# Opening of an attention and feed-forward kernel: products that alternate between heads, a second transposed buffer, another order of loads

## The chip, the cores and the metric

The kernel runs on one core of a Trainium2 chip. Its time is device microseconds of one execution. Three executions of the kernel before took 940.44, 939.76 and 935.5 us (median 939.76). The profile is of one more execution.

A core has five engines with queues of their own: PE (matrix products; its weight loads are listed as PEld), DVE (vector), ACT (scalar), POOL (GpSimd) and SP, which here only issues DMAs. PE writes to PSUM, which has banks of 512 columns of 4 bytes; DVE and ACT read PSUM and SBUF, POOL works in SBUF.

## The reference

Masked attention for 8 batches and 8 heads (576 positions, 64 columns each), then a feed-forward layer with a gate over all 4608 positions:

```python
scores = scale * np.matmul(q, k.transpose(0, 1, 3, 2))
mask_local = (rel >= 0) & (rel < stride)
mask_strided = (rel >= 0) & (pos[None, :] % stride == pos[:, None] % stride)
...
scores = scores - np.max(scores, axis=-1, keepdims=True)
attn = np.exp(scores)
attn = attn / (np.sum(attn, axis=-1, keepdims=True) + 1e-09)
...
h = x @ w_in
relu6 = np.clip(h + 3.0, 0.0, 6.0)
g = h * relu6 / 6.0
return (g @ w_out).astype(np.float32)
```

The stride is 32. Heads 0 to 3 use the local mask, heads 4 to 7 the strided one. The feed-forward layer goes from 512 columns to 2048 and back.

## The kernel before

**Pairs and chunks.** Heads are worked two at a time. A pair g is batch b and chunk c (0 to 3, two heads each); chunks 0 and 1 are local, 2 and 3 strided. In batch 0 the order of the chunks is 0, 2, 1, 3. The text calls them pair 0, pair 2, pair 1 and pair 3, by their chunk; names of tiles carry batch and chunk: `ps_00` is a score bank of batch 0, chunk 0.

**A pair.** Queries and keys are loaded, transposed, and multiplied to scores in two PSUM banks, one per head. A masking product with the identity lies below them. Then come the maximum of each row, its subtraction, the exponential, the sum, its inverse, and the normalising product. The probabilities are transposed and multiplied with the values (`pv`), and `keep_x` (L401) splits the result into a high and a low part, `x`, for the feed-forward products; ACT casts the high part, DVE subtracts to get the low one. The last 64 positions of each batch go to tiles `left`.

The code of `kept_pair` (L427) serves the pairs of batches 0 and 1; later pairs have `pair` (L774). Within `kept_pair`, the pairs of batch 0 are `early`: they load and transpose queries and keys on PE (L475, L482), have more PSUM banks to choose from, and take the maximum straight from PSUM, negated (`most_of`, L619). PE then adds that to the scores in the bank (`less_of`, L622), and ACT reads the bank for the exponential (`exp_of`, L626). Local pairs of batch 0 are also `shifted`: their probabilities are transposed on PE (`turned`, L705), and copied back (L710, L712) to a tile `at`. Their products with the values (`both`, L714) run over one head, 18 blocks of 32 positions, then over the other. Strided pairs transpose their probabilities on DVE (L693), each head into the same zeroed tile `atkept`: the second head's transposes follow the first head's products (`mm`, L743).

**Feed-forward.** For each batch's 512 main positions, and for the left ones, 16 hidden chunks: `ph` gets four groups of three products (high and low parts of x and w_in, L1033 to L1035; one group for each chunk c of x), ACT and DVE apply the gate, ACT and POOL split it (`gh`, L1057, and `gl`, L1062), and three products per output bank go into `acc` (L991 to L993). For batch 0, the first four hidden chunks are begun together.

**Weights.** `weight_part` (L293) loads each 128x512 piece (L306) and splits it: two ACT passes (L314, L318), a DVE join (L322), a cast on ACT or POOL (L328, L330), a subtraction on POOL (L334).

**Order.** `Plan` (L54) collects all operations with their costs and due times, and `emit` (L84) writes them out in the order in which a list schedule with these costs would start them. So costs and due times decide what stands where on each engine's queue, and any change of them can move rows anywhere behind it. Engines work their queues in order. The calls that the change touches give due times to loads (`op("SP", ...)`, L336, L497, L542). Where the plan sees PE idle early, it puts in idle products (`idle`, L1134).

Of the kernel before, what the change touches and what calls it, by code (L numbers as in the profile page):

```python
# [33 lines left out]
TURNS = ((0, 2, 1, 3), (2, 3, 0, 1)) + ((0, 2, 1, 3),) * 6  # L34
AHEAD = 27.0
# [139 lines left out]
def attention_ffn(ctx: ExitStack, tc, q, k, v, w_in, w_out, out):  # L175
# [117 lines left out]
    def weight_part(k, w, g, i):  # L293
# [42 lines left out]
        op("SP", 0.53, load, writes=[key], due=-49 + 0.01 * k if k < 6 else -2 + 0.1 * k if k < 16 else due - 20.0, early=7.0 if k < 16 else due - 30.0, after=1.6 if k < 16 else 1.25)  # L336
# [90 lines left out]
    def kept_pair(g):  # L427
# [7 lines left out]
        slow = 1.7 if g == 0 else 1.1 if early else 1.0  # L435
# [26 lines left out]
        for x in "qk":  # L462
# [6 lines left out]
            if early:  # L469

                def load(x=x, nkey=nkey):
                    t = new(wp, nkey, [P, RUN, 2, D], F32, f"{x}n{nm}")
                    rows = {"q": q, "k": k}[x][b, h0:h0 + 2].rearrange("j (p i) d -> p i j d", i=RUN)
                    for part in (slice(0, D), slice(D, S // RUN)):
                        (nc.scalar if g == 1 else nc.sync).dma_start(t[part], rows[part])  # L475
# [21 lines left out]
                op("ACT" if g == 1 else "SP", 0.9, load, writes=[nkey], due=-60 + 2 * g + (x == "k") - 900 * (g == 1), after=1.15)  # L497
                op("PE", 0.126 * RUN * (1.1 if g else 1.6), tr, words=4 * RUN, reads=[("ident",), nkey, "plain", tkey[x]], writes=tb, take=tb, due=due - 1020, mode="s")
# [43 lines left out]
        op("SP", 1.8 if loc else 2.0, load_v, writes=[vkey, skey] if shifted else [vkey], due=-48.8 if g == 1 else -54.5 + 2 * g if early else due - 30, early=0 if early else due - 35, after=3.0 if shifted else 2.0)  # L542
# [3 lines left out]
        akeys = [("atl", j) for j in range(2)] if loc else [wkey("o", NQ - 1, 0)] * 2  # L546
# [50 lines left out]
        def keep(e, j):  # L597
# [3 lines left out]
            if e == "ACT":  # L601
                nc.scalar.copy(e_both()[:, j], ps)
            else:
                nc.vector.tensor_copy(e_both()[:, j], ps)
        both_halves = [x + (1,) if isinstance(x, tuple) else x + "1" for x in (qkey, kkey)]
        sd = due - 12
        op("PE", (2.0 if loc else 1.75) * slow, scores, reads=["const", qkey, kkey, *both_halves], writes=[*sb, stkey] if early else [*sb, ekey, ekey + "1", stkey],
           take=sb, due=sd - 1000, room=0.0 if early else ROOM, mode="s", words=4 * 2 * (18 if loc else 32) + 6)
        for j in range(0 if early else 2):
# [6 lines left out]
        def most_of(j):  # L616
            if j == 0:
                new(ap, stkey, [P, 2, 2, 8], F32, f"st{nm}")
            nc.vector.tensor_reduce(out=st_of(0)[:, j], in_=ps_of(j), axis=AX.X, op=ALU.max, negate=True)  # L619

        def less_of(j):
            nc.tensor.matmul(ps_of(j), tiles["ident",][:n, :n], st_of(0)[:, j].unsqueeze(2).to_broadcast([n, nblk, w]),  # L622
                             start=False, stop=True, skip_group_check=True)

        def exp_of(j):
            nc.scalar.activation(e_own(j), in_halves(ps_of(j)), AF.Exp, scale=SCALE)  # L626
# [29 lines left out]
        if early:  # L656
            for j in range(2):
                op("DVE", 0.18 + 0.00105 * cols, partial(most_of, j), reads=[sb[j]], writes=[stkey] if j == 0 else [stkey + (1,)], due=sd + 0.7)
            for j in range(2):
                op("PE", 0.0018 * cols * slow, partial(less_of, j), reads=[stkey if j == 0 else stkey + (1,), ("ident",)], writes=[sb[j]], due=sd - 999, mode="l", words=4)  # L660
            for j in range(2):
                op("ACT", 0.2 + 0.00085 * cols, partial(exp_of, j), reads=[sb[j]], writes=[ekey] if j == 0 else [ekey + "1"], give=sb[j], due=sd + 1.5)
# [19 lines left out]
        def transposes(j):  # L682
            def tr():
                at, e = tiles[akeys[j]], e_whole(j)
# [10 lines left out]
            op("DVE", 6 * 0.37 if loc else 4 * 0.435, tr, reads=[ekey, ekey + "1"], writes=[akeys[j]], due=due - 2 + j)  # L695
# [478 lines left out]
```

## Time and profile before

| | |
|---|---|
| median of 3 runs | 939.76 us |
| the profiled execution's own time | 940.2 us |
| its span, first to last instruction | 938.4 us |
| mean granted PE clock | 0.993 |
| POOL, share of the span | 44% |
| DVE, share of the span | 63% |
| moved by DMA | 57.60 MB, 61 GB/s over the span |

In the tables by stage and in the timelines, times are us from the span's start. A timeline row has the start, the length, the engine, the line, the operation, what is written and read with its size, the count of merged instructions, and in brackets the idle time before and what ended it. A busy PE may be running products that take longer than their work needs, so its 98% is no measure of what could be saved.

### The profile page before, as it was taken

Reading aid. Unit: us, or ns where it says so; the run is one execution under the profiler, and the core shown is the slowest. Engines: PE = TensorE matmul, PEld = TensorE weight load, DVE = VectorE, ACT = ScalarE, POOL = GpSimd, SP = SyncE. Lnnn points to the kernel's source line nnn. Section 1 sums busy time; section 2 is a strip of 40 time slices with the busy share of each in tenths; the row PEclk is TensorE's granted clock in tenths of the full one; section 3 lists DMA queues with packets and bytes.
Section 4 is the critical chain, followed back from the end, with each engine's and each line's share of the span. In section 5 each row is a group of like instructions: output and inputs, shape, how many; then the busy total and the mean of one; then the engine's idle time right before and its main releaser. Section 6 shows DMA issues by size and latency. Waiting matters only on the chain.

```text
span 938.4 us, 16352 instructions
## 1 busy us (share of the span) xinstructions
PE 922.1 (98%) x5741; PEld 762.4 (81%) x5741; DVE 590.3 (63%) x1604; ACT 491.0 (52%) x1214; POOL 417.0 (44%) x398
## 2 busy tenths in 40 slices
PE   7989999999999999999999999999999999999997
PEld 5778788888888888988888888888888888888896
DVE  4677968677877765556476778777887675111111
ACT  1657657655565546456356555655556563322332
POOL 3468675544444434433354444454454452222221
PEclk9979999999999999999999999999999999999999
DMA  9978522321222022023013222322223200100100
GB/s 147 329 164 240 144 58 43 77 49 29 53 71 42 15 56 71 1 49 55 14 29 84 40 42 40 83 44 42 40 42 78 49 1 14 45 1 1 39 8 23
DMA packets 194394, 57.60 MB, mean 61 GB/s; under 512 B 185032, under 2 KB 185032, under 8 KB 194312
## 3 DMA queue, kind: packets, MB, share of 16 engines
q1 hardware_dynamic: 191960, 55.97, 26.3%
q10 hardware_dynamic: 2352, 0.59, 0.4%
q8 instruction: 45, 0.74, 0.3%
q14 instruction: 37, 0.30, 0.1%
HBM read 47.09 MB, written 9.44 MB: 60 GB/s over the span
## 4 chain that ended last, share of the span: by engine, by line
PE 93%; DMA 2%; SPq 2%; DVE 1%; issue 1%; POOL 1%; ACT 0%; POOLq 0%
PE acc L991 13%; PE ph L1033 13%; PE acc L993 12%; PE acc L992 12%; PE ph L1034 12%; PE ph L1035 12%; PE ps L868 3%; PE pv L398 2%; PE phl L1033 2%; PE phl L1035 2%; PE phl L1034 2%; PE accl L993 2%; PE accl L991 2%; PE accl L992 2%; PE pv L943 1%
## 5 line engine op out<-in xcount | busy, mean ns | idle before, releaser
L1062 POOL TENSOR_TENSOR gl<-u,gh 128x512 fp32r<-128x512 f32 x128 | 169.8, 1327 | 267.1 <-ACT gh L1057 242.8
L1033 PE MATMUL ph<-x,wi 128*128 128x512 f32 x512 | 202.2, 395 | 0.0
L991 PE MATMUL acc<-wo,gh 128*128 128x512 f32 x512 | 202.1, 395 | 0.0
L993 PE MATMUL acc<-wo,gl 128*128 128x512 f32 x512 | 200.2, 391 | 0.3 <-POOL gl L1062 0.3
L1034 PE MATMUL ph<-x,wi 128*128 128x512 f32 x512 | 200.2, 391 | 0.0
L1035 PE MATMUL ph<-x,wi 128*128 128x512 f32 x512 | 200.0, 391 | 0.0
L992 PE MATMUL acc<-wo,gh 128*128 128x512 f32 x512 | 199.8, 390 | 0.0
L1045 ACT ACTIVATE u<-ph,three 128x512 f32<-128x512 f32 x128 | 88.2, 689 | 190.9 <-PE ph L1035 190.0
L1049 DVE SCALAR_TENSOR_TENSOR u<-u,ph 128x512 f32<-128x512 f32 x128 | 87.6, 685 | 126.5 <-ACT u L1045 124.9
L892 ACT ACTIVATE e<-e,st 96x128 f32<-96x128 f32 (+2 forms) x264 | 102.7, 391 | 43.9 <-DVE st L886 43.3
L993 PEld LDWEIGHTS acc<-wo,gl 128*128 128x128 f32 x512 | 96.1, 188 | 22.0 <-POOL gl L1062 1.3
L1035 PEld LDWEIGHTS ph<-x,wi 128*128 128x128 f32 x512 | 96.4, 188 | 20.7
L991 PEld LDWEIGHTS acc<-wo,gh 128*128 128x128 f32 x512 | 96.1, 188 | 19.6
L1033 PEld LDWEIGHTS ph<-x,wi 128*128 128x128 f32 x512 | 96.4, 188 | 18.9 <-DVE u L1049 0.5
L992 PEld LDWEIGHTS acc<-wo,gh 128*128 128x128 f32 x512 | 96.2, 188 | 17.8
L1034 PEld LDWEIGHTS ph<-x,wi 128*128 128x128 f32 x512 | 96.5, 188 | 16.7
L1057 ACT CAST gh<-u 128x512 fp32r<-128x512 f32 x128 | 79.3, 621 | 57.3 <-DVE u L1049 52.0
L908 POOL TENSOR_TENSOR e<-e,st 96x96 f32<-96x96 f32 (+1 forms) x72 | 68.4, 963 | 81.1 <-DVE st L903 74.9
L886 DVE CUSTOM_DVE_ANT_0 e<-ps,e 96x128 f32<-96x128 f32 (+2 forms) x264 | 63.4, 279 | 2.2
L925 DVE STREAM_TRANSPOSE atstr<-e 32x160 f32<-32x160 f32 x168 | 56.3, 335 | 7.2 <-POOL e L908 4.5
L925 DVE STREAM_TRANSPOSE atloc<-e 32x192 f32<-32x192 f32 (+1 forms) x144 | 52.1, 362 | 9.4 <-POOL e L908 7.1
L418 DVE TENSOR_TENSOR x<-pv,x 128x512 fp32r<-128x512 f32 (+3 forms) x48 | 31.7, 660 | 36.6 <-ACT x L415 24.2
(154 smaller groups left out, 1378.6 us busy)
## 6 DMA issues: line engine op xcount, KB each, us to landing
rawi<-in_moe_w_in_dram SPq DMA_DIRECT2D x16, 512.0 KB
rawo<-in_moe_w_out_dram SPq DMA_DIRECT2D x16, 512.0 KB
out_dram<-ob SPq DMA_DIRECT2D x32, 256.0 KB
qn<-in_q_dram SPq DMA_DIRECT2D x112, 72.0 KB
kn<-in_k_dram SPq DMA_DIRECT2D x112, 72.0 KB
vt<-in_v_dram SPq DMA_DIRECT2D x24, 160.0 KB
vt<-in_v_dram SPq DMA_DIRECT2D x120, 31.5 KB
v<-in_v_dram SPq DMA_DIRECT2D x16, 72.0 KB
```

Source lines behind the costliest of these rows:

```text
L892: nc.scalar.activation(e, e, AF.Exp, bias=st_of(j, 0)[:, i:i + 1], scale=-1.0, accum_out=st_of(j, 1)[:, i:i + 1])
L925: nc.vector.transpose(at[ks, i0:, qs], e[qs, i0:, ks])
L991: nc.tensor.matmul(acc, gh, woh, start=fc == 0, stop=False)
L992: nc.tensor.matmul(acc, gh, wol, start=False, stop=False)
L993: nc.tensor.matmul(acc, gl, woh, start=False, stop=end)
L1033: nc.tensor.matmul(ph, wih, xh, start=n_ == 0, stop=False)
L1034: nc.tensor.matmul(ph, wih, xl, start=False, stop=False)
L1035: nc.tensor.matmul(ph, wil, xh, start=False, stop=n_ == NCC - 1)
L1045: nc.scalar.activation(u, tiles[pk][:, :n], AF.Relu, bias=three)
L1049: nc.vector.scalar_tensor_tensor(out=u, in0=u, scalar=6.0, in1=tiles[pk][:, :n], op0=ALU.min, op1=ALU.mult)
L1057: nc.scalar.copy(g, tiles[uk][:, :n])
L1062: eng.tensor_tensor(out=g, in0=tiles[uk][:, :n], in1=tiles[gk[0]][:, :n].bitcast(F32), op=ALU.subtract)
```

## The change

Five things change, all for the pairs of batch 0.

- **Products with the values.** In local pairs, `both` now takes blocks of the two heads in turn. Each bank gets 9 blocks of either head (288 positions) in place of 16 and 2. `keep_x` reads the banks in three pieces.
- **A second buffer for strided pairs.** The second head's probabilities go to two tiles of their own (`at1`), zeroed once on DVE, so both heads' transposes may precede all products, which `both_mm` issues in turn by head. Eight transposes of 128 columns are issued for the second head in place of four of 256.
- **Maximum and subtraction.** Scores are copied from PSUM to SBUF (`keep`, as in later pairs). The maximum is taken there, POOL subtracts it, and the exponential works in place. PE's L622 products are gone. Local pairs do this by head, strided pairs for both heads at once.
- **Loads.** Due times of loads come from lists. SP's queue now has the queries of pairs 0 and 2, the values of pair 0, two pieces of w_in, queries and keys of pair 1, two more of w_in, the values of pair 2, queries and keys of pair 3, the values of pair 1. ACT issues the keys of pairs 0 and 2, where it issued queries and keys of pair 2. Before, the queries and keys of all four pairs and the values of pairs 0 and 1 stood ahead of the first weight.
- **Costs** in the plan of early pairs and loads.

The diff, cut to its core:

```diff
+FIRST = (-57.0, -53.9, -56.5, -53.8)
+QK = (-60.0, -59.0, -55.0, -52.0)
+VAL = (-56.0, -53.0, -51.0, -49.0)
...
-        slow = 1.7 if g == 0 else 1.1 if early else 1.0
+        slow = (1.75, 1.75, 1.6, 1.3)[g] if b == 0 else 1.0
...
-                        (nc.scalar if g == 1 else nc.sync).dma_start(t[part], rows[part])
+                        (nc.scalar if g < 2 and x == "k" else nc.sync).dma_start(t[part], rows[part])
...
         def most_of(j):
-            if j == 0:
-                new(ap, stkey, [P, 2, 2, 8], F32, f"st{nm}")
-            nc.vector.tensor_reduce(out=st_of(0)[:, j], in_=ps_of(j), axis=AX.X, op=ALU.max, negate=True)
+            nc.vector.tensor_reduce(out=st_of(0)[:, j].rearrange("p (h u) -> p h u", h=2), in_=e_own(j), axis=AX.X, op=ALU.max)
 
         def less_of(j):
-            nc.tensor.matmul(ps_of(j), tiles["ident",][:n, :n], st_of(0)[:, j].unsqueeze(2).to_broadcast([n, nblk, w]),
-                             start=False, stop=True, skip_group_check=True)
+            x = e_own(j)
+            nc.gpsimd.tensor_tensor(out=x, in0=x, in1=in_halves(st_of(0)[:, j].unsqueeze(2).to_broadcast([n, nblk, w])), op=ALU.subtract)
...
-        if early:
+        if shifted:
             for j in range(2):
...
+                if akeys[j] == "at1":
+                    for a in range(4):
+                        rows = slice(PAD * a, PAD * a + PAD)
+                        for h in range(2):
+                            nc.vector.transpose(tiles["at1", h][rows, :, rows], e[rows, 4 * h:4 * h + 4])
+                    return
...
-                for j in range(2):
-                    own = slice(D * j, D * j + D)
-                    for u in range(3 * NQB):
-                        n0 = PAD * u
...
+                half = 3 * NQB // 2
+                for h in range(2):
+                    for x in range(half):
+                        for j in (h, 1 - h):
+                            own = slice(D * j, D * j + D)
+                            bank = (h + j) % 2
+                            u = x + half * bank
+                            n0 = PAD * u
...
+            def both_mm():
+                ps, vt = [psum(vb[h], f"pv{nm}{h}") for h in range(2)], tiles[vkey]
+                for i in range(8):
+                    for j in range(2):
+                        at = tiles["at1", i // 4][:, i % 4] if j else tiles[akeys[0]][:, i]
+                        nc.tensor.matmul(ps[i // 4][D * j:D * j + D, i % 4 * P:i % 4 * P + 4 * NPOS], vt[:, j, i],
+                                         at.rearrange("p (a m) -> p a m", a=4)[:, :, :NPOS], start=True, stop=True)
...
+    def at1(e):
+        for h in range(2):
+            t = tiles["at1", h] = new(xp, ("x", 1, 2, h), [P, 4, P], F32, f"at1{h}")
+            on(e).memset(t, 0.0)
+    op(either(1.1), 0, at1, writes=["at1", ("x", 1, 2, 0), ("x", 1, 2, 1)], due=9)
```

How rows move, at three places. The numbers of lines are each kernel's own. PE at pair 0's products with the values, before (`pv_00` and `pv_01` are the two banks):

```order
L722 MATMUL pv_00_510<-at_0_466,v_0_179 64x32 x16
L722 MATMUL pv_01_511<-at_0_466,v_0_179 64x32
L722 MATMUL pv_01_511<-at_0_466,vlast 64x32
L722 MATMUL pv_00_510<-at_0_466,v_0_179 64x32 x16
L722 MATMUL pv_01_511<-at_0_466,v_0_179 64x32
```

and now, where pair 1's scores already stand ahead of them:

```order
L486 MATMUL qp_30_543<-ident,qn_3_315 128x72 x4
L486 MATMUL qp_31_544<-ident,qn_3_315 128x72 x4
L734 MATMUL pv_00_568<-at_0_458,v_0_172 64x32
L734 MATMUL pv_01_569<-at_0_458,v_0_172 64x32
L734 MATMUL pv_00_568<-at_0_458,v_0_172 64x32
L734 MATMUL pv_01_569<-at_0_458,v_0_172 64x32
```

One head's 18 blocks in a row have become blocks of two heads in two banks by turns.

POOL from the normalising of pair 0's probabilities on (`e`; `st_2` are the row values of pair 2, `st_1` those of pair 1; `wi` and `fi` are pieces of w_in), before:

```order
L634 TENSOR_TENSOR e<-e,st_0_328 96x2x3x64 x2
L458 MEMSET qt_2_456 128x32x14
L653 TENSOR_TENSOR e<-e,st_2_451 128x2x8x18
L330 CAST wi_555<-fi_483 128x512
L522 MEMSET v_2_605 128x1024
L334 TENSOR_TENSOR wi_555<-fi_483,wi_555 128x512
```

and now:

```order
L636 TENSOR_TENSOR e<-e,st_0_307 96x2x3x64 x2
L462 MEMSET qt_2_423 128x32x14
L640 TENSOR_TENSOR e<-e,st_2_417 128x2x8x18
L333 CAST wi_430<-fi_405 128x512
L337 TENSOR_TENSOR wi_430<-fi_405,wi_430 128x512
L337 TENSOR_TENSOR wi_451<-fi_425,wi_451 128x512
L655 TENSOR_TENSOR e<-e,st_2_417 128x2x8x18
L625 TENSOR_TENSOR e<-e,st_1_561 96x2x3x64
L333 CAST wi_622<-fi_520 128x512
L625 TENSOR_TENSOR e<-e,st_1_561 96x2x3x64
L526 MEMSET v_2_646 128x1024
L337 TENSOR_TENSOR wi_622<-fi_520,wi_622 128x512
```

The subtractions of the maximum (L640, L625) are new here; two weights and pair 1's subtractions have come ahead of the memset of `v`.

DVE from the transposes of pair 2's probabilities on, before:

```order
L693 STREAM_TRANSPOSE atkept<-e 32x8x32 x4
L322 SCALAR_TENSOR_TENSOR fi_483<-fi_483,rawi_258 128x512
L418 TENSOR_TENSOR x_01_600<-pv_00_510,x_00_599 128x512
L418 TENSOR_TENSOR left_0_82<-pv_01_511,left_0_81 128x64
L322 SCALAR_TENSOR_TENSOR fi_550<-fi_550,rawi_304 128x512
L619 TENSOR_REDUCE st_1_685<-ps_10_557 96x6
```

and now (`at_179` and `at_181` are the second buffer, which takes eight rows by turns):

```order
L701 STREAM_TRANSPOSE atkept<-e 32x8x32 x4
L690 STREAM_TRANSPOSE at_179<-e 32x4x32
L690 STREAM_TRANSPOSE at_181<-e 32x4x32
...
L621 TENSOR_REDUCE st_1_561<-e 96x6
L325 SCALAR_TENSOR_TENSOR fi_520<-fi_520,rawi_289 128x512
L621 TENSOR_REDUCE st_1_561<-e 96x6
L325 SCALAR_TENSOR_TENSOR fi_534<-fi_534,rawi_291 128x512
```

Pair 1's maximum now follows both heads' transposes of pair 2 directly, ahead of pair 0's `x`.

More of the change, by code (lines that the diff above doesn't have):

```diff
@@ L496, in evac @@
                         nc.vector.tensor_copy(to, ps)
-                op("ACT" if g == 1 else "SP", 0.9, load, writes=[nkey], due=-60 + 2 * g + (x == "k") - 900 * (g == 1), after=1.15)
-                op("PE", 0.126 * RUN * (1.1 if g else 1.6), tr, words=4 * RUN, reads=[("ident",), nkey, "plain", tkey[x]], writes=tb, take=tb, due=due - 1020, mode="s")
+                op("ACT" if g < 2 and x == "k" else "SP", 1.7, load, writes=[nkey], due=QK[g] + 0.1 * (x == "k") - 900 * (g < 2 and x == "k"), after=1.7)
+                op("PE", 0.7 * slow, tr, words=2 * RUN, reads=[("ident",), nkey, "plain", tkey[x]], writes=tb, take=tb, due=due - 1020, mode="s")
                 for h in range(2):
@@ L655, in kept_pair @@
         red = 0.18 + 0.0019 * cols
-        if early:
+        if shifted:
             for j in range(2):
-                op("DVE", 0.18 + 0.00105 * cols, partial(most_of, j), reads=[sb[j]], writes=[stkey] if j == 0 else [stkey + (1,)], due=sd + 0.7)
-            for j in range(2):
-                op("PE", 0.0018 * cols * slow, partial(less_of, j), reads=[stkey if j == 0 else stkey + (1,), ("ident",)], writes=[sb[j]], due=sd - 999, mode="l", words=4)
-            for j in range(2):
-                op("ACT", 0.2 + 0.00085 * cols, partial(exp_of, j), reads=[sb[j]], writes=[ekey] if j == 0 else [ekey + "1"], give=sb[j], due=sd + 1.5)
+                ej, sj = (ekey + "1", stkey + (1,)) if j else (ekey, stkey)
+                op("DVE", 0.18 + 0.00095 * cols, partial(most_of, j), reads=[ej, stkey], writes=[sj], due=sd + 0.7)
+                op("POOL", pool / 2 + 0.05, partial(less_of, j), reads=[sj], writes=[ej], due=sd + 1)
+                op("ACT", 0.2 + 0.00085 * cols, partial(exp_of, j), writes=[ej], due=sd + 1.5)
         else:
@@ L715, in both @@
                 ps, at, vt = [psum(vb[h], f"pv{nm}{h}") for h in range(2)], tiles[akey], tiles[vkey]
-                for j in range(2):
-                    own = slice(D * j, D * j + D)
-                    for u in range(3 * NQB):
-                        n0 = PAD * u
-                        u1 = max(u, 1) - 1
-                        vu = vt[own, u1] if u1 < TOK // PAD else tiles["atl", 1][own, odd]
-                        nc.tensor.matmul(ps[n0 // TOK][own, n0 % TOK:n0 % TOK + PAD], vu, at[own, n0:n0 + PAD], start=True, stop=True)
@@ L723, in kept_pair @@
-            op("PE", 0.15 * NQB * slow, turned, reads=[("ident",), ekey, ekey + "1"], writes=[*tb, akey, akey + ("b",)], take=tb, due=due - 1002, mode="s", words=4 * NQB)
+                half = 3 * NQB // 2
[6 more added lines that the diff above has]
+                            n0 = PAD * u
+                            u1 = max(u, 1) - 1
+                            vu = vt[own, u1] if u1 < TOK // PAD else tiles["atl", 1][own, odd]
+                            nc.tensor.matmul(ps[bank][own, PAD * x:PAD * x + PAD], vu, at[own, n0:n0 + PAD], start=True, stop=True)
```

37 lines of the change are left out of this document (24 added, 13 removed).

## The prediction

> **What bounds the kernel now.** I read the page's busy shares first, then the busy time of each engine by stage, then the timeline of each engine over the first 75 us. The page's first row, and the stages (stretch in us, its length, then busy us of PE, PEld, DVE, ACT and POOL with their counts, granted PE clock, DMA share, GB/s):
>
> ```profile
> PE 922.1 (98%) x5741; PEld 762.4 (81%) x5741; DVE 590.3 (63%) x1604; ACT 491.0 (52%) x1214; POOL 417.0 (44%) x398
> ...
> 0.00:40.00 40.00, 34.14 (x575) 26.40 (x575) 19.65 (x39) 12.76 (x27) 13.31 (x39) 1.00 0.98 214
> 40.00:57.80 17.80, 13.60 (x128) 11.85 (x127) 13.19 (x26) 11.17 (x25) 11.88 (x13) 0.84 0.93 270
> 57.80:72.30 14.50, 14.50 (x199) 11.50 (x199) 11.57 (x22) 9.01 (x19) 10.61 (x14) 0.84 0.66 168
> 72.30:140.00 67.70, 66.99 (x616) 53.43 (x615) 52.46 (x91) 42.85 (x79) 51.00 (x46) 1.00 0.55 141
> 140.00:800.00 660.00, 659.98 (x3560) 546.70 (x3559) 474.58 (x1395) 375.98 (x994) 298.56 (x258) 1.00 0.22 45
> ```
>
> From 57.8 us on PE has no gap worth the name (0.7 us in the next 82, none from 140 to 800). What the change takes from the opening is therefore taken from the end, if PE stays dense afterwards. I measure the opening by one mark: the end of the 16 groups of three products that make the first four hidden chunks (ph_0 to ph_3, four x parts each). Rows of PE around it (start, length, line, operation):
>
> ```profile
> 49.27 0.71 PE L705 MATMUL pt<-ident,e 96*128 96x96 f32 x6
> ...
> 68.14 0.30 PE L580 MATMUL ps<-mtri,eye 128*128 128x144 bf16 x2
> ...
> 69.56 0.50 PE L1033 MATMUL ph<-x,wi 128*128 128x512 f32 x1
> ...
> 72.20 0.39 PE L1035 MATMUL ph<-x,wi 128*128 128x512 f32 x1
> ```
>
> The last of the 16 groups starts its last product at 72.20, and the pitch between such products is about 0.24 (twelve from 69.56 to 72.20), so a group costs 0.7 and the mark stands at 72.4. Scores of batch 1 lie before it from 68.14 to 69.56; the new order has them behind the mark, so the comparable mark of before is **71.0**.
>
> **The value products.** Before, all 18 of one head come first, then all 18 of the other; each matmul leaves two records:
>
> ```profile
> 27.03 3.86 PE L722 MATMUL pv<-at,v 64*64 64x32 f32 x36
> 30.68 0.29 PE L722 MATMUL pv<-at,vlast 64*64 64x32 f32 x1
> 30.71 0.29 PE L722 MATMUL pv<-at,v 64*64 64x32 f32 x1
> 30.79 0.29 PE L722 MATMUL pv<-at,vlast 64*64 64x32 f32 x1
> 30.82 3.49 PE L722 MATMUL pv<-at,v 64*64 64x32 f32 x31
> 34.12 0.40 PE L722 MATMUL pv<-at,vlast 64*64 64x32 f32 x2
> ```
>
> 72 records from 27.03 to about 34.45 is 103 ns each. At the one place where the heads meet, records of both interleave: 30.68 and 30.79 of one, 30.71 and 30.82 of the other. So each head keeps its own step of 0.11, and two heads run beside each other. The new order does that throughout: 72 x 0.103 / 2 = **3.7 us**, a saving of 3.7 per pair, in two pairs. Bounds: no saving (7.4), or the step of the scores, which also alternate heads:
>
> ```profile
> 7.89 2.15 PE L482 MATMUL qp<-ident,qn 72*128 72x72 f32 x16 [2.14 <-DMA qn<-in_q_dram]
> 12.03 2.15 PE L482 MATMUL kp<-ident,kn 72*128 72x72 f32 x16 [1.99 <-DMA kn<-in_k_dram]
> ...
> 14.97 1.52 PE L591 MATMUL ps<-kplain,qplain 64*32 64x64 f32 x72
> ...
> 17.43 2.80 PE L622 MATMUL ps<-st,ident 96*96 96x384 f32 x4
> ```
>
> That gives 1.5. I take 3.7, since it is read from these very matmuls. keep_x now cuts the result in three: one more cast on ACT and one more subtraction on DVE, 0.2 each, beside PE work.
>
> **The loads.** SP and ACT issue all four loads of pairs 0 and 2 first, and the first weights ahead of pairs 1 and 3. Rates while small pieces move, and while weights move, and the first weight's arrival:
>
> ```profile
> 5.00:10.00 5.00, 2.86 (x18) 1.97 (x16) 2.04 (x5) 0.90 (x2) 2.90 (x9) 1.00 1.37 156
> 25.00:30.00 5.00, 5.00 (x43) 4.86 (x42) 3.63 (x9) 2.91 (x9) 0.76 (x2) 1.00 1.01 384
> ...
> 27.41 0.66 ACT L314 ACTIVATE fi<-rawi 128x512 f32<-128x512 f32 x1 [1.90 <-DMA rawi<-in_moe_w_in_dram]
> ```
>
> Before, 3.47 MB of heads (22.2 us at 156 GB/s) and 0.52 MB of weights (1.4) lie ahead of 27.41: an offset of 3.8. With it, the 1.18 MB of pairs 0 and 2 are there at 11.4 (12.03 before), two weights at 17.7, pair 1 at 21.4, pair 3 at 28.7. Pair 3 and the values of pair 1 are later than before by some 6 us (2.1 MB of weights and 0.3 MB of values are moved ahead); they are used at 27 and 43, so what they lose is covered.
>
> **The softmax and the second buffer.** Two PE matmul groups of L622 per early pair go; the maximum is now read from SBUF after a copy, and GpSimd subtracts. Rows of DVE, ACT and POOL:
>
> ```profile
> 16.56 1.02 DVE L619 TENSOR_REDUCE st<-ps 96x6 f32<-96x384 f32 x2 [2.36 <-PE ps L591]
> 19.51 0.55 DVE L630 TENSOR_REDUCE st<-e 96x6 f32<-96x384 f32 x1 [1.38 <-ACT e L626]
> 21.63 0.15 DVE L648 TENSOR_TENSOR st<-st,eps 96x12 f32<-96x12 f32 x1
> 27.34 1.79 DVE L693 STREAM_TRANSPOSE atkept<-e 32x256 f32<-32x256 f32 x4 [0.54 <-POOL e L653]
> 29.16 0.69 DVE L322 SCALAR_TENSOR_TENSOR fi<-fi,rawi 128x512 int32<-128x512 int32 x1
> 35.49 1.63 DVE L322 SCALAR_TENSOR_TENSOR fi<-fi,rawi 128x512 int32<-128x512 int32 x1
> 102.99 0.55 DVE L604 COPY e<-ps 96x384 f32<-96x384 f32 x1
> ```
>
> ```profile
> 18.99 0.49 ACT L626 ACTIVATE e<-ps 96x384 f32<-96x384 f32 x1 [1.40 <-PE ps L622]
> ```
>
> ```profile
> 22.20 1.62 POOL L634 TENSOR_TENSOR e<-e,st 96x384 f32<-96x384 f32 x2 [14.00 <-DVE st L649]
> 23.75 0.47 POOL L458 MEMSET qt<- 128x448 f32 x1
> 26.64 0.67 POOL L653 TENSOR_TENSOR e<-e,st 128x288 f32<-128x288 f32 x1 [2.42 <-DVE st L649]
> 29.92 0.61 POOL L330 CAST wi<-fi 128x512 fp32r<-128x512 f32 x1 [2.60 <-DVE fi L322]
> 34.37 0.95 POOL L522 MEMSET v<- 128x1024 f32 x1 [3.84 <-DMA v<-in_v_dram]
> 35.28 1.29 POOL L334 TENSOR_TENSOR wi<-fi,wi 128x512 fp32r<-128x512 f32 x1
> ```
>
> The wait of the memset at 34.37 is put on a DMA, but the tile it clears is read by the products that end at 34.45: the slow products hold POOL, and POOL holds the weights behind it. Also, a DVE join (L322) takes 0.69 alone, and 1.63 at 35.49, when POOL's subtraction runs to 36.57: it ends 0.55 after that. DVE's two-input operations and POOL's take turns. [...] Without the turns the sum below would be 2.2 us better (three joins of 0.69 and an inverse of 0.15).
>
> Subtracting costs 0.81 per head on POOL and 0.67 for a whole strided pair. The second strided buffer needs 8 narrower transposes in place of 4. The nearest row:
>
> ```profile
> L925 DVE STREAM_TRANSPOSE atstr<-e 32x160 f32<-32x160 f32 x168 | 56.3, 335 | 7.2 <-POOL e L908 4.5
> ```
>
> No such row has 128 columns: between 0.22 (half of the 0.45 for 256 columns, 1.79 / 4) and 0.335; I take 0.30, so 2.4 for 1.79. Clearing the buffer (128x512, twice) stands on DVE before its first copy at about 9 us, where it was idle: nothing. What goes is the wait to refill one buffer between the two heads.
>
> **The sum.** Us from the span's start:
> - Pair 0's scores: q2 there 11.4, half of a 2.15 transposition group 1.1, scores 2.3 (14.18 to 16.49 before): 14.8.
> - Copy 0.55, two maxima 1.0, the second subtraction 1.1, exponential 0.5, sum 0.55, inverse 0.4, normalising 1.6, hops 0.3: 20.9 (23.8 before).
> - POOL's row from there: memset 0.47, one DVE join 0.69, pair 2's subtraction 0.67, cast 0.61, two subtractions of weights 2.6, normalising pair 2 0.67: 26.6.
> - DVE then transposes pair 2 into both buffers, 1.8 + 2.4: 30.8. **Pair 1's maximum is queued behind these.**
> - Pair 1: maximum 0.5, subtraction 0.8, and, by turns, two joins 1.4, the second maximum and subtraction 1.3, then POOL's memset 0.95, two weight subtractions 2.6, the inverse between them 0.15, normalising 1.6: 40.1.
> - PE then: transposes 1.1 (49.27 before), two groups 1.4, products 3.7: 46.3. Five groups 3.4; 0.8 for DVE to finish pair 3's transposes; its products 1.2; four groups 2.7; 0.8 for the split of x part 3; four groups 2.7: **57.9**.
>
> So 71.0 - 57.9 = 13.1 us less, of which some 2.3 are the halved clock (0.16 of 14.5 us in the stage from 57.8). The profiled execution took 940.2 us for a span of 938.4, and the median of the runs shown is 0.4 below it: 940.2 - 13.1 = 927.1, and **926.7** as a median. A measurement of this kernel can tell about 0.5% from no change.
>
> **Rivals.**
> - *More comes off:* no turns between DVE and POOL (2.2), products at the scores' step (2.2 of pair 1), transposes at 0.22 (0.6), pair 0's loads at 10.0, right behind the first transpositions (1.4): 920.3, and 918 with 2 for links that overlap where I lay them end to end. Against it stands 35.49.
> - *The products keep 103 ns:* pair 1's cost 3.7 more, and pair 0's end holds POOL's memset 0.8 more: 931.2. Against it stands the interleaving at 30.7.
> - *The clock halves again:* before, it lost 2.3 us in the stage from 57.8; the same, or as much over the whole opening: 929 to 932. [...]
> - *POOL sets the pace:* its row is full from 31 to 70 us, and the first low part of a hidden chunk, by the same counting, is ready at 58.5 against 59.3, when PE wants it. Three us of stalls: 930. Together with the one above: 935, no change that can be measured.
> - *Slower:* the changed loads and costs make the planner write another order for all engines nearly to the end. 28 pairs of batches 1 to 7 are woven into the dense stretch. If in each PE waits 0.65 us for POOL's subtraction, that is 18 us, and 945. The point is 0.47 us for a pair, where nothing is gained. Now all waits there are 0.7 together and POOL is busy 45% of 140 to 800, so this is unlikely.
> - *The change does not do what it says* (loads in new order, but the same landing): pair 0 at 12.03, 0.6 us: 927.3, inside the forecast.
>
> **How the numbers follow.** The forecast with its errors (922 to 932) 0.58; more comes off 0.14; products unchanged, or clock or POOL, 932 to 935, 0.12; several of them at once, 935 to 944, 0.11; slower 0.05. Faster by over 0.5% (below 935) 0.84, within 0.11, slower 0.05. The range from 918 to 935 leaves out some 0.18.
>
> **What would show it.** Value products of pair 0 in 3.7 us; PE's transposes of pair 1 near 40 and the mark near 58; POOL without gap from 31; DVE's join longer than 0.69 beside POOL's subtractions; PE's gaps after 60 under 1 us in sum. Wrong it is if pair 1's maximum does not wait for pair 2's transposes, if the clock falls in the opening, or if PE waits from 140 to 800.

## The result, and the profile after

The changed kernel takes **932.4 us** (median of 6 runs, 931.6 to 937.1), the kernel before 939.4 (6 runs, 935.5 to 940.4): a ratio of 0.9936, with a 95% interval from 0.9919 to 0.9953. It is faster: by 7.0 us between the medians, by 0.6% in that ratio. This lies inside the range of 918 to 935, but 13.1 us and a median of 926.7 were forecast. The profiled run took 932.27 us for a span of 930.5.

The first row of the page, and the stages, with the prediction's columns (stretch, length, busy us of PE, PEld, DVE, ACT and POOL with counts, granted PE clock, DMA share, GB/s):

```profile
PE 907.8 (98%) x5731; PEld 750.5 (81%) x5731; DVE 578.6 (62%) x1607; ACT 495.8 (53%) x1224; POOL 434.1 (47%) x409
```

```profile
0.00:40.00 40.00, 27.73 (x471) 21.15 (x471) 23.72 (x53) 16.16 (x36) 21.09 (x47) 0.64 1.08 188
40.00:62.90 22.90, 19.08 (x292) 15.32 (x288) 16.98 (x38) 14.61 (x32) 17.72 (x21) 0.88 0.96 277
...
72.30:140.00 67.70, 66.89 (x618) 53.79 (x617) 53.36 (x93) 44.61 (x82) 52.38 (x45) 1.00 0.57 139
140.00:800.00 660.00, 659.96 (x3561) 547.12 (x3560) 457.53 (x1382) 376.21 (x995) 304.50 (x263) 1.00 0.22 46
```

From 140 to 800 us PE is as dense as before (0.04 us idle), so the whole difference lies in the opening. In its first 40 us PE is busy for 27.7 us, where it was busy for 34.1 before. What it waits for in the first 75 us (waits of PE: total us, times, longest):

```profile
PE qp L486 <- DMA qn<-in_q_dram: 5.3, 3, 3.0
PE ps L595 <- issue: 3.8, 1, 3.8
PE ph L1059 <- POOL wo L333: 3.6, 1, 3.6
```

The same in PE's timeline (start, length, line, operation, and in brackets the idle time ahead of it and what ended it by the profile):

```profile
12.88 1.19 PE L486 MATMUL qp<-ident,qn 72*128 72x72 f32 x8 [1.82 <-DMA qn<-in_q_dram]
...
18.65 1.00 PE L595 MATMUL ps<-kplain,qt 64*32 64x18 f32 x97
23.44 0.44 PE L595 MATMUL ps<-kplain,qt 64*32 64x18 f32 x31 [3.79 <-issue]
...
28.39 0.80 PE L584 MATMUL ps<-mband,eye 96*96 96x384 bf16 x2 [1.44 <-DVE kplain L500]
...
40.48 1.46 PE L595 MATMUL ps<-kt,qt 64*32 64x18 f32 x128
45.55 0.59 PE L1059 MATMUL ph<-x,wi 128*128 128x512 f32 x1 [3.62 <-POOL wo L333]
...
46.79 1.16 PE L713 MATMUL pt<-ident,e 96*128 96x96 f32 x6
...
62.67 0.39 PE L1061 MATMUL ph<-x,wi 128*128 128x512 f32 x1
```

The last row is the last product of the 16 groups: the mark is at 62.9 (forecast 57.9, before 71.0). 71.0 - 62.9 = 8.1, and the span is 7.9 shorter, so the mark measures what it should, and it comes **5.0 us late**. Two rows hold more than that between them: PE stops in the middle of pair 2's scores, between two products of one group, where the profile shows nothing that it waits for, and again ahead of the first hidden chunk. The second stop is put on a cast of GpSimd, but that cast writes an output weight, and the weights of the waiting product had been loaded into PE at 41.86:

```profile
41.86 0.29 PEld L1059 LDWEIGHTS ph<-x,wi 128*128 128x128 f32 x1
45.56 0.29 PEld L1060 LDWEIGHTS ph<-x,wi 128*128 128x128 f32 x1 [3.40 <-issue]
```

So both are stops of PE's issue. What PE lacks is instructions. The rows of the DMA queues, of the whole span and of the stretch from 20 to 21 us (packets, MB, share):

```profile
q8 instruction: 45, 0.74, 0.3%
```

```profile
q8 instruction: 1, 0.02, 8.9%
```

45 packets bring 0.74 MB, 16 KB each; PE has 5731 products and as many weight loads, and 11462 / 45 is 255 instructions for a packet. In the trace 449 instructions of PE, a few semaphore instructions among them, lie ahead of the first stop and 1217 ahead of the second: 768 apart, three times 256. A packet starts at 20.48, 0.8 after the first stop begins, takes 1.4, and PE goes on at 23.44; the packet at the second stop starts at 43.25, 1.3 after that stop begins.

The traces of all kernels of this text bear this out. In their first 75 us the profiles mark 19 stops of PE of 1 us and more with "issue". Counted in the same way, 449, 705, 961, 1217, 1473 or 1985 instructions lie ahead of each of them, always 193 more than a multiple of 256; 1217 also lie ahead of the two that the profile puts on a cast of GpSimd, here and in the third kernel below. The strided scores of a pair are 128 products and as many weight loads in the trace, 256 instructions in some 1.5 us, and use up a block faster than any other code of this kernel. The planner counts these instructions ("words") too, with 3.2 us at the least from the end of one block to the end of the next. That was too little here: from the begin of the block ahead of each stop until PE went on it took 7.7 us (15.74 to 23.44) and 5.1 us (40.48 to 45.55).

```python
WORDS = 256
REFILL = 3.2
...
while held >= WORDS:
    held -= WORDS
    free[e] = end = turned = max(end, turned + REFILL)
```

### The profile page after: what moved, and what is told of

Same layout as the page of the kernel before. It is cut to its first block, busy times and chain, and to the rows that moved or that the text cites. A ratio compares the mean times of both kernels' runs of the same rounds, so it can differ in the third digit from the quotient of the medians.

```text
span 930.5 us, 16361 instructions
## 1 busy us (share of the span) xinstructions
PE 907.8 (98%) x5731; PEld 750.5 (81%) x5731; DVE 578.6 (62%) x1607; ACT 495.8 (53%) x1224; POOL 434.1 (47%) x409
## 4 chain that ended last, share of the span: by engine, by line
PE 94%; DMA 2%; issue 1%; SPq 1%; POOL 1%; DVE 1%; ACT 0%; POOLq 0%
PE acc L1017 13%; PE acc L1019 13%; PE ph L1059 13%; PE acc L1018 13%; PE ph L1060 12%; PE ph L1061 12%; PE ps L894 3%; PE pv L402 2%; PE phl L1059 2%; PE phl L1061 2%; PE phl L1060 2%; PE accl L1019 2%; PE accl L1017 2%; PE accl L1018 2%; PE pv L969 1%; DMA qn<-in_q_dram 1%
## 5 line engine op out<-in xcount | busy, mean ns | idle before, releaser
L1075 DVE SCALAR_TENSOR_TENSOR u<-u,ph 128x512 f32<-128x512 f32 x128 | 87.6, 685 | 129.5 <-ACT u L1071 128.4
L1018 PEld LDWEIGHTS acc<-wo,gh 128*128 128x128 f32 x512 | 96.2, 188 | 17.8
L839 POOL TENSOR_TENSOR qq<-qt,qq 64x576 fp32r<-64x576 f32 x31 | 45.5, 1466 | 30.4 <-ACT qq L835 15.7
L951 DVE STREAM_TRANSPOSE atloc<-e 32x192 f32<-32x192 f32 (+1 forms) x144 | 52.1, 362 | 11.7 <-POOL e L934 9.3
```

The source lines that it names most:

```text
L951: nc.vector.transpose(at[ks, i0:, qs], e[qs, i0:, ks])
L1018: nc.tensor.matmul(acc, gh, wol, start=False, stop=False)
L1075: nc.vector.scalar_tensor_tensor(out=u, in0=u, scalar=6.0, in1=tiles[pk][:, :n], op0=ALU.min, op1=ALU.mult)
```

## The experiments

Times are medians; "before" was run beside each on the same chip (938.7 to 939.9). The mark below is the start of the last product of the 16 groups in the profiled run (after: 62.67; before: 72.2, with batch 1's scores ahead of it).

**1 and 2. Where the blocks of instructions end.** Tiny products, two instructions each, ahead of everything; the order behind them is the same.

```diff
     warm[0] = pp.tile([P, TOK], F32, tag="ph_1", name="idle")
+    for i in range(32):      # 96 in the second kernel
...
+        nc.tensor.matmul(warm[0][out, :NPOS], eye[own, :PAD], eye[own, :NPOS], start=True, stop=True)
```

> The changed kernel with 32 tiny PE products (64 instructions with their weight loads) ahead of everything, before the first idle products; the order of all else is the same. Theory A (PE's instructions arrive in blocks of 256, and PE stands still when it has used up a block before the next one is there): both long stops of PE move with the count of instructions. The first goes from behind 97 records of pair 2's scores to behind some 65, the second from the first ph product to behind some 96 records of pair 3's scores; each still 2 to 4 us; span 929 to 931. Theory B (PE waits there for work of other engines, as the views put it): both stops stay at the same instructions; span 930.5.

> The same with 96 tiny products, 192 instructions. Theory A: the ends of blocks fall at the start of pair 2's scores and at 32 records into pair 3's, with the next block asked for long before; both stops shrink from 3.8 and 3.6 us to under 1 each; span 923 to 925. Theory B: no change, 930.5, or somewhat later by the time of the tiny products.

With 64 instructions the first stop comes 32 products earlier, behind 65 of pair 2's scores, as theory A had it; the second is gone, where A had 2 to 4 us in pair 3's scores. PE's timeline of that kernel:

```profile
18.50 0.84 PE L595 MATMUL ps<-kplain,qt 64*32 64x18 f32 x65
21.45 0.84 PE L595 MATMUL ps<-kplain,qt 64*32 64x18 f32 x63 [2.11 <-issue]
```

928.95 us (one run), mark at 58.7. With 192, pair 2's scores run through, and two shorter stops stand elsewhere (2.2 in pair 1's transposition, 1.1 in its value products): 929.05 us (925.9 to 932.9), ratio 0.9906 (0.9871 to 0.9940), mark at **56.9**, which is earlier than forecast. The time missed theory A's 923 to 925. With more work to do the median is 3.4 us below the changed kernel's, though the intervals of the two ratios overlap. The stops moved with the number of instructions that were added: they are ends of blocks, and no wait for data.

**3 and 4. The alternation, undone in the change and done alone.**

```diff
-for h in range(2):
-    for x in range(half):
-        for j in (h, 1 - h):
+for j in range(2):
+    for h in (j, 1 - j):
+        for x in range(half):
```

> The changed kernel with the local pairs' products one head after the other again, in the same two banks, so with the same count of instructions and all else in the same order. If alternating is what makes them short: 7 us for each pair, in place of 4.0 (at half clock) and 2.2 (at full clock); span 935 to 938. If the two banks or the place do it: 930.5.

> The kernel before with nothing changed but the products' order: the two heads in turn, in the banks they had. By the prediction's step (products 3.7 us a pair, and GpSimd's memset no longer held): pair 0's products end 4 to 5 us earlier, pair 1's take 2 to 4; 930 to 934. If the other parts of the change carry the gain: 937 to 940.

The change without the alternation took 939.44 us (one run), as before: pair 0's products took 7.4 us (after: 4.0), pair 1's 4.7 (2.2). The alternation alone, in the old banks, took **934.15** us (934.06 to 934.47), ratio 0.9947 (0.9929 to 0.9965). One swap of two loops in the kernel before thus brings 5.7 us, where the whole change brings 7.0; as the blocks lie in the changed kernel, the other four edits add 1.3. The prediction had split its 13.1 into 7.4 for the alternation and 5.7 for the rest.

**5. The same four edits, with the blocks shifted.** The third kernel, with 192 instructions ahead.

> The changed kernel with the value products head after head again, and 96 tiny products (192 instructions) ahead of everything. Without those 192 instructions it took 939.4 us, no less than before, so the other four edits seemed to be worth nothing. Theory A (the other four edits do bring time, but two stops of TensorE for its instructions take it back): the stop in pair 2's scores goes, as it did in the changed kernel, and the time falls by 3 to 6, to 933.5 to 936.5. Theory B (the other four edits are worth nothing by themselves; the stops are only idle time that TensorE would have anyway): the stops move, and the time stays at 938.5 to 940.5.

933.4 us (932.8 to 936.1), ratio 0.9944 (0.9927 to 0.9961), just below the band of theory A: the four edits do bring 5.5 us once the blocks end elsewhere. Theory B falls.

**6 and 7. Another place for the first stop, and products in the gaps.** 128 instructions ahead; in the seventh kernel ten of the products are large and stand in PE's gaps ahead of the transpositions of q0 and q2.

> The changed kernel with 64 tiny products (128 instructions) ahead of everything. Theory A (blocks of 256 instructions, fetched some 5 us after the block before them is begun): the first block's end falls 33 records into pair 2's strided scores, with the begin of that block now ahead of pair 0's scores, so the stop there is 0 to 1 us (3.8 without, 2.1 with 64 instructions); the next block's end falls in pair 1's transpositions, where TensorE waits for a load anyway. 925 to 929. Theory B (the place of the first stop does not matter, since the loads set the pace): as with 64 or 192 instructions, 929 to 930.

> The same 128 instructions, but 10 of the products are of 128x512 and stand in the two gaps of TensorE ahead of the transpositions of q0 and q2 (five each), so that no gap there is over 1.5 us. Clock theory: the first fall of the granted clock (10.24 us) does not come; transpositions, scores and the value products of pair 0 up to the next gap run at full clock, and the time is 2 to 4 below that of the kernel with 128 instructions and no large products. Rival (the loads bind while the clock is halved): the clock stays up, and the time is within 1 us of that kernel's. Other rival (the fall has nothing to do with these gaps): the clock falls all the same.

932.65 (932.3 to 932.9) and 931.8 us (930.2 to 933.2). In the sixth kernel the first stop went as theory A said, and no stop is left ahead of the first chunk, but neither of the two times came (925 to 929, 929 to 930): PE now waits there for loads, 7.4 us in sum.

```profile
22.03 1.11 PE L486 MATMUL qp<-ident,qn 72*128 72x72 f32 x8 [2.35 <-DMA qn<-in_q_dram]
...
25.23 1.19 PE L486 MATMUL kp<-ident,kn 72*128 72x72 f32 x8 [2.09 <-DMA kn<-in_k_dram]
...
32.65 1.19 PE L486 MATMUL qp<-ident,qn 72*128 72x72 f32 x8 [2.96 <-DMA qn<-in_q_dram]
```

So the first stop of the changed kernel lies beside loads of pairs 1 and 3 that are as late. The mark came 1.7 us earlier (61.0), and a stop of 1.2 us behind the mark, at 71.2, took part of that back. In the seventh kernel no gap before 20 us is over 1.82, and the clock was halved at 12.4 all the same; the clock theory missed.

**8. The loads as before.** All else of the change stays.

```diff
-due=FIRST[k] if k < 4 else -49.2 + 0.01 * k if k < 6 else ...
+due=-49 + 0.01 * k if k < 6 else ...
...
-(nc.scalar if g < 2 and x == "k" else nc.sync).dma_start(t[part], rows[part])
+(nc.scalar if g == 1 else nc.sync).dma_start(t[part], rows[part])
...
-op("SP", 3.9 if shifted else 1.5, load_v, ..., due=VAL[g] if early else due - 30, ...)
+op("SP", 1.8 if loc else 2.0, load_v, ..., due=-48.8 if g == 1 else -54.5 + 2 * g if early else due - 30, ...)
```

> The changed kernel with the order, the queues and the planner's costs of the loads (weights, queries and keys, values) as before. Theory A (the order of loads does little by itself, as the prediction's last rival has it: 0.6 us at pair 0): 931 to 935, within 2.5 us of the changed kernel. Theory B (apart from the alternation, the loads are what the change brings): 936 to 939, with pair 0's scores over 2 us later.

**928.5 us** (928.4 to 930.0), ratio 0.9890 (0.9875 to 0.9905), the lowest median of all: both theories had expected a slower kernel. With the old order of loads the change is 4 us faster. How much of that is the loads themselves was not separated from the stops, which are 6.2 us shorter here: with the new loads and other ends of blocks the second kernel came to 929.05. PE's timeline:

```profile
16.93 1.22 PE L485 MATMUL qp<-ident,qn 72*128 72x72 f32 x8
17.94 1.17 PE L485 MATMUL kp<-ident,kn 72*128 72x72 f32 x8
...
20.51 0.67 PE L594 MATMUL ps<-kplain,qt 64*32 64x18 f32 x43 [0.17 <-issue]
...
24.43 0.85 PE L583 MATMUL ps<-mband,eye 96*96 96x384 bf16 x2
...
32.81 1.10 PE L594 MATMUL ps<-kt,qt 64*32 64x18 f32 x89 [0.97 <-issue]
...
39.32 1.16 PE L712 MATMUL pt<-ident,e 96*128 96x96 f32 x6
```

Pair 1's heads are transposed at 16.9 without a wait (23.8 in the changed kernel), between pair 0's scores and pair 2's; the stops are 0.2 and 1.0; pair 1's scores start at 24.4 (28.4), its transposes at 39.3 (forecast 40.1, changed kernel 46.8), and the mark stands at 56.9.

**9 and 10. The two other edits, one at a time,** with alternation and the loads as before: without the second buffer, and without the subtraction on GpSimd.

```diff
-... [wkey("o", NQ - 1, 0), "at1" if early else wkey("o", NQ - 1, 0)]
+... [wkey("o", NQ - 1, 0)] * 2
...
```

```diff
-nc.gpsimd.tensor_tensor(out=x, in0=x, in1=..., op=ALU.subtract)
+nc.tensor.matmul(ps_of(j), tiles["ident",][:n, :n], st_of(0)[:, j]..., start=False, stop=True, skip_group_check=True)
...
```

> The kernel with the loads as before (928.5 us), and with one strided buffer as before: alternating products and the maximum subtracted on GpSimd are left of the change. The alternation alone took 934.2. Theory A (the second buffer is worth the wait to refill the one buffer between two heads, 1.5 us of TensorE before, in two strided pairs): 930 to 932. Theory B (the subtraction on GpSimd brings nothing, the second buffer all of the 5.7): 933.5 to 935. Theory C (the second buffer brings nothing): within 1 us of 928.5.

> The kernel with the loads as before (928.5 us), and with the maximum read from PSUM and subtracted on TensorE as before: alternating products and the second strided buffer are left. Theory A (the subtraction on GpSimd takes some 3 us out of pair 0's path and four groups of some 0.7 off TensorE): 931 to 933. Theory B (DVE and GpSimd taking turns cost what it saves): 927.5 to 929.5. Theory C (it brings all of the 5.7): 933.5 to 935.

943.5 us (ratio 1.0044, 1.0023 to 1.0065) and 934.4 us (0.9961, 0.9945 to 0.9976), beside 934.2 with neither and 928.5 with both. The tenth is where its theory C had it; no expectation had this for the ninth. The edits work only as a pair. By the code, the reason is a buffer: scores that are copied out of PSUM at once need the probabilities' buffer `e` at once, and with one transposed buffer `e` stays held until the first head's products are done and the second head is transposed. The timeline agrees. Pair 3's scores, at 30.9 with both, start at 45.8, behind these (DVE's timeline of the ninth kernel):

```profile
40.76 1.79 DVE L700 STREAM_TRANSPOSE atkept<-e 32x256 f32<-32x256 f32 x4 [1.27 <-PE pv L774]
```

**11. The loads alone,** in the kernel before.

> The kernel before with the changed order, queues and planner's costs of the loads and nothing else. Theory A (the new order costs time by itself, since strided scores come closer behind other small products and TensorE stops for instructions): stops marked issue of over 3 us in sum ahead of the first chunk, 941 to 944 against 939. Theory B (the order does little by itself): 937.5 to 940. Theory C (it brings what the prediction held, 0.6 and more): below 937.5.

944.0 us (939.1 to 946.5), ratio 1.0049 (1.0029 to 1.0070): slower by some 4.6 us, about as much as the same order costs in the changed kernel, and again with stops in it. The time is at the upper end of theory A's; of the stops, 1.2 lie in pair 2's scores and 2.5 in its products, so only the first is where it was expected.

**12. Pair 0's scores first.** In the changed kernel they stand behind the transposition of q2, which waits for its load to 12.88.

```diff
-..., due=due - 1020, mode="s")
+..., due=due - 1020, mode="s", room=2.0 if g == 1 and x == "q" else 0.0)
```

> The changed kernel with one thing else: the transposition of pair 2's queries is planned 2 us later, so that pair 0's scores stand ahead of it on TensorE and do not wait for that load; the order behind is nearly the same. Theory A (the path from pair 0's scores sets the opening, and the block of instructions whose end stops pair 2's scores is begun earlier, so its successor is there sooner): pair 0's scores start by 12.5 instead of 13.9, the stop in pair 2's scores is under 2.8 instead of 3.8, and the time is 928.5 to 931. Theory B (pair 2's scores and the second stop set the opening): 931.5 to 933.

936.6 us (933.2 to 939.7), a miss. Pair 0's scores start at 9.2 and the first stop is gone, but PE waits 4.3, 1.3 and 2.8 us for loads of pairs 1 and 3, and the second stop is still there (3.35), with the mark at 62.9.

**13 and 16. The second stop alone.** 48 tiny products ahead of pair 2's value products, and 96 ahead of the transposition of pair 3's queries.

> The changed kernel with 48 tiny products (96 instructions) just ahead of pair 2's value products, where TensorE runs an idle product anyway; all before that, the first stop too, stays. The end of the block that stopped the first product of ph moves 80 records into pair 3's scores, and its begin ahead of pair 2's value products, so that the next block has 5 us to come. Theory A (the second stop, 3.6 us, is on the path: it delays the first chunk, pair 1's transposes and with them the mark): no stop over 1 us there, the 16 groups' last product at about 60 instead of 62.7, and 929 to 930.5. Theory B (loads and the softmax of pair 1 set the path, and the stop lies beside them): the stop goes, a wait of TensorE for DVE, GpSimd or a load takes its place, and the time is 931.5 to 933.

> The changed kernel with 96 tiny products (192 instructions) between pair 1's scores and the transposition of pair 3's queries; all ahead of them, the first stop too, stays. The block that ended at the first product of ph ends 32 records into pair 3's scores, and begins ahead of pair 0's value products, 7 us before. So far the kernels with a stop of 2.8 to 3.6 us between pair 3's scores and the first chunk had the mark at 62.7 to 63.0, and those without it at 56.9 to 61.0. Theory A (the second stop is the missing term of the prediction's sum, the first one lies beside the late heads): the first stop stays at about 3.8, no stop over 1 us ahead of the first chunk, mark at 58.5 to 60, and 928.5 to 930.5. Theory B (both kinds come from something else, such as late weights): the first chunk starts at 45 all the same, waiting for an engine or a load, and 931.5 to 933.5.

In the thirteenth kernel the stop moved to where it was expected, into pair 3's scores, but stayed 3.0 long: 933.1 us (931.5 to 934.7), mark at 62.8. The guess of 5 us for the next block to come was too short there (it took 7.2 from the block's begin). In the sixteenth it went, and the first one stayed:

```profile
22.88 0.44 PE L598 MATMUL ps<-kplain,qt 64*32 64x18 f32 x31 [3.88 <-issue]
...
40.10 1.47 PE L598 MATMUL ps<-kt,qt 64*32 64x18 f32 x128
41.50 0.56 PE L1062 MATMUL ph<-x,wi 128*128 128x512 f32 x1
```

The first chunk starts at 41.5 instead of 45.55, the mark is at 58.6, and the time is 930.5 us (927.7 to 931.6), ratio 0.9909 (0.9886 to 0.9932). Theory A holds for the mark; the time is at the edge of its band, and its interval overlaps that of the changed kernel. The clock does not explain the earlier mark: the changed kernel ran at half clock from 45.5 to 49.0 and this one at full from 41.7, but from the start of the first chunk to the mark both took 17.1 us.

**14 and 15. Pair 1's heads ahead of the first weights,** alone and with the twelfth kernel's order.

```diff
-FIRST = (-57.0, -53.9, -56.5, -53.8)
+FIRST = (-54.5, -53.9, -54.4, -53.8)
```

> The changed kernel with the first two weights planned behind pair 1's queries and keys instead of ahead of them; nothing else of the order of loads is undone. Theory A (pair 1's heads come too late in the changed order, and with the old order of all loads the kernel took 928.5): pair 1's scores start by 26 instead of 28.4, and 929 to 931. Theory B (the place of the blocks of instructions alone decides): the two stops together are as long as before (some 7 us) and the time is 931.5 or more, or they are shorter and it is below, whatever pair 1's scores do.

> The two orders together: pair 0's scores ahead of the transposition of pair 2's queries (936.6 alone, where TensorE then waited 4.3, 1.3 and 2.8 us for loads of pairs 1 and 3), and the first two weights behind pair 1's queries and keys (930.8 alone). Theory A (the first order lost because pair 1's heads came too late, not by itself): waits for loads of pair 1 under 2 us in sum, pair 1's scores by 23, and 926 to 929.5. Theory B (pair 1's heads are not what the first order lost by): 931 or more, with pair 1's scores no earlier than 23.2.

Alone 930.75 us (928.0 to 933.2): pair 1's scores start at 23.2, both stops are under 0.5, the mark is at 57.3. Together 938.0 (934.8 to 941.6), a miss of theory A, though the waits for pair 1's loads fell to 2.4 in sum and its scores start at 23.1. The planner now put both transpositions of pair 3 ahead of pair 0's products and five idle products ahead of pair 2's, and the second stop is back (2.76): mark at 63.0. What each of the two costs was not tried.

The marks of the kernels that keep alternation, second buffer and subtraction, side by side, fall in two groups:

| kernel | stop within pair 3's scores or the first chunk, or between them, us | mark, us |
|---|---|---|
| changed; 12; 13; 15 | 3.6; 3.4; 3.0; 2.8 | 62.7; 62.9; 62.8; 63.0 |
| 1; 2; 6; 7 | none there (0.7 to 1.1 later in 2, 6 and 7) | 58.7; 56.9; 61.0; 57.8 |
| 8; 14; 16 | 1.0; none (1.7 of waiting for a weight); none | 56.9; 57.3; 58.6 |

The clock does not sort them so: it is full for good from 39.2 us in the fifteenth kernel (mark 63.0) and only from 49.9 in the seventh (57.8). Each mark is that of one run. The profiled runs of 2, 14 and 16 are the fastest of their kernels, some 3 us below the median, so the medians differ by less than these marks.

## Why the prediction was wrong, point by point

- **The step that failed** is "the sum": PE's rows laid end to end, as if each could start when its data are there. It has no term for PE's instructions. Followed along its own links, pair 0's scores ended at 16.4 (forecast 14.8; the load of q2 was there at 12.9, not 11.4), pair 2's normalising at 30.2 (26.6; GpSimd's memset waited 1.4 for the scores that the first stop held), and pair 1's at 42.9 (40.1). What PE's transposes of pair 1 need was then there, but they stood behind the first chunk and its stop, and began at 46.79, **3.9 us** later. The rows from there to the mark ran 1.7 faster than forecast (16.1 for 17.8; pair 1's products took 2.2, not 3.7): 2.8 + 3.9 - 1.7 = 5.0.

```profile
24.06 0.47 POOL L462 MEMSET qt<- 128x448 f32 x1 [1.42 <-PE ps L595]
...
29.57 0.67 POOL L655 TENSOR_TENSOR e<-e,st 128x288 f32<-128x288 f32 x1
...
41.26 1.61 POOL L636 TENSOR_TENSOR e<-e,st 96x384 f32<-96x384 f32 x2
```

  With the second stop taken away alone (sixteenth kernel), the transposes started at 42.75, right behind that row (there to 42.70), and the mark stood 4.1 us earlier. That was the fastest run of that kernel; between the medians it is 1.9 us (932.4 and 930.5). So that the second stop lies on the path is shown; what it costs in time is known only as some 2 to 4 us. The code counts these instructions, with its `WORDS` and `REFILL`, and the prediction makes no use of those lines. In the changed kernel's opening two ends of blocks hold PE for 3.8 and 3.6 us; at the other four up to the mark (behind 193, 705, 961 and 1473 instructions) it goes on within 0.01 us.
- **The loads** were the second thing wrong in that sum. "Pair 3 and the values of pair 1 are later than before ...; what they lose is covered" holds for the values; the heads of pairs 1 and 3 are not covered. PE waits for them as soon as the first stop is gone (2.4, 2.1 and 3.0 us in the sixth kernel, 4.3, 1.3 and 2.8 in the twelfth). The prediction had pair 1 landing at 21.4; its keys came to 25.2 there. It also had pair 3 landing at 28.7 and used at 27, so by its own numbers that was not covered. The rival of 927.3, "loads in new order, but the same landing", was too kind to the new order: pair 0's scores began at 13.87, and at 13.98 before, so nothing was gained there, and the change takes 928.5 with the old order and 932.4 with the new one, stops included.
- **Alternation:** the mechanism is right. Pair 0's products took 3.98 us (forecast 3.7), pair 1's 2.2, at full clock. Two heads run beside each other: 55 ns for a record at half clock and 31 at full, where head after head gave 103 and 65.
- **GpSimd's subtraction and the second buffer:** together worth 5.7 us with the old loads (934.15 to 928.5), about what the sum had for all that is not alternation. That the size agrees is partly luck, since the sum had put earlier loads into it; that the two edits need each other was not said.
- **The turns** of DVE and GpSimd are there, as the rows of both show (alone DVE's join takes 0.69 and GpSimd's subtraction of the maximum 0.82):

```profile
34.13 0.55 DVE L621 TENSOR_REDUCE st<-e 96x6 f32<-96x384 f32 x1
34.60 0.68 DVE L325 SCALAR_TENSOR_TENSOR fi<-fi,rawi 128x512 int32<-128x512 int32 x1
...
43.01 1.45 DVE L325 SCALAR_TENSOR_TENSOR fo<-fo,rawo 128x512 int32<-128x512 int32 x1
...
57.84 1.81 DVE L325 SCALAR_TENSOR_TENSOR fi<-fi,rawi 128x512 int32<-128x512 int32 x1
```

```profile
34.76 1.37 POOL L625 TENSOR_TENSOR e<-e,st 96x384 f32<-96x384 f32 x1 [4.52 <-DVE st L621]
...
43.24 0.67 POOL L640 TENSOR_TENSOR e<-e,st 128x288 f32<-128x288 f32 x1
...
57.81 1.30 POOL L337 TENSOR_TENSOR wo<-fo,wo 128x512 fp32r<-128x512 f32 x1
```

  The prediction has them for DVE's two-input operations as such; that is too wide: the gate product `u`, which reads `ph` from PSUM, took 0.70 at most in all its 128 rows (L1075, median 0.69), with GpSimd's subtractions beside it or not.

  Pair 1's maximum (34.13) stands right behind the transposes into the second buffer (32.08 to 34.1; 2.03 us, forecast 2.4), as the sum had it, some 3 us late by then.
- **The clock:** the prediction read 1.00 for the opening of before. That number is not a measurement there: the record of the clock begins at 38.5 us, and the rows ahead of it have the lengths of half clock. Eight transpositions take 0.69 us at full clock (first kernel, 8.10, clock 0.95 in that stretch) and 1.19 at half; before, sixteen took 2.15. After, the record has half clock for 10.24 us from 8.0, for 20.48 from 21.6 and for 3.41 from 45.5; before, for 10.24 from 52.1. So both kernels run most of the opening at half clock, and "the clock falls in the opening" was no test. After, it is full for good from 49.0 us, before from 62.4, so the part of the path for which the sum counted on 2.3 us did run at full clock.

```profile
8.10 0.69 PE L486 MATMUL qp<-ident,qn 72*128 72x72 f32 x8 [1.76 <-DMA qn<-in_q_dram]
```

- **PE's gaps and the clock:** in the trace after, half clock begins beside the longest gaps of PE (from 8.0, within the gap of 3.03, from 21.6, within that of 3.79, and from 45.5, at the end of that of 3.62); in the seventh kernel it begins at 12.4, with gaps of 1.81 at most until then. So what brings the clock down was not shown.
- **The rivals:** "the clock halves again" (929 to 932) and "the products keep 103 ns" (931.2) come near the time for the wrong reason: the products took 55 and 31 ns, and the clock was half in the opening of before too. The stated range holds the time, but not for a cause that it was made from. "GpSimd sets the pace" did not come: its row has gaps of 4.5 us ahead of 34.76 and 3.0 ahead of 49.45, where it should have been full from 31, and it holds PE for 0.3 us between 60 and 140. "Slower" did not come: PE idles 0.04 us from 140 to 800.

## What to carry to other kernels

Where a stretch of code issues hundreds of small instructions in a microsecond or two, count them: in these kernels the next block came late (3.8 and 3.6 us of stop in the changed kernel) when such a burst stood at a block's begin, and a few harmless instructions ahead of it, or other work between, moved the mark by up to 6 us, though not in all of them (the thirteenth). A load that is moved ahead is paid by those moved back, and a stop elsewhere can hide that; undo each part of a change by itself before keeping it. Here the change with the old order of loads beats both kernels: 928.5 us.

## What the runs showed of the hardware

- PE's instructions come in packets of some 256 (45 packets for 11462), and the stops stand 256 or a multiple of it apart; in the changed kernel one is on its way 0.9 to 1.6 us, and at the two stops PE goes on 1.3 and 1.5 us after it has landed. By the count above, in the first 60 us of the changed kernel its transfer started 0.5 to 6.1 us after PE began the block ahead of it. What sets that stays open, and with it why the times of some kernels scatter (925.9 to 932.9 in the second).
- The mean granted clock of an execution says little here. Of 26 runs of the kernel before on one chip, 11 at 0.988 or more had a median of 939.4 us, 15 at 0.983 or less 939.2: where the record begins late (at 38.5 us in the profile of before), its first part is given as full.
